# Attention and two gated layers on one core: casts and subtractions of converted weights put off behind the next step's split, and conversions moved between steps

## Chip, cores and metric

The kernel runs on one core of a Trainium2 chip. The metric is the device time of one execution in microseconds. The engines named below are PE (TensorE: matmuls), DVE (VectorE), ACT (ScalarE), POOL (GpSimd) and SP (SyncE, which issues DMAs).

## What is computed

Local attention feeds a gated layer, whose result feeds a second one with products in a row. All weights come as 64-bit floats; all arithmetic is float32.

```python
attn = softmax(masked(q @ k.T / sqrt(64))) @ v        # 4 x 8 heads x 576 x 64
x = attn.transpose(0, 2, 1, 3).reshape(2304, 512)
x = (silu(x @ w_gate) * (x @ w_val)) @ w_out          # d_ff = 1536
x = (((x @ w1) * (x @ w2)) @ w3) @ w_out2             # d_ff = 1024
```

## The kernel before

**Products.** A float32 value is held as two parts, `hi` (rounded, type fp32r) and `lo` (the rest). A product is the sum of three matmuls, hi x hi, hi x lo and lo x hi. `w3 @ w_out2` is multiplied out once (`fold_mm`) to a folded weight `fw`, so the second layer too is "up" products, an elementwise product and one "down" product.

**Slices and steps.** The features of both layers are cut into 20 slices of 128: slices 0 to 11 are the first layer's, 12 to 19 the second's. The 2304 tokens are cut into groups 0 to 3 of 512 and group 4 of 256. A step (c, g) is slice c with group g. On PE a step is the up product of (c, g), twice 12 matmuls into the banks `pa` and `pb`, and then the down product of the step before, 12 matmuls into the banks `po`. The down product of (c, g) so stands behind the up product of the step after. DVE multiplies `pr` = `pb` x `ga`, ACT having made `ga` from `pa` (silu, or a copy in the second layer); ACT casts `pr` to `sh`, POOL subtracts `sl` = `pr` - `sh` (`split_act`). The first matmul of the down product reads `sh`, the second `sl`. DVE adds the four `po` banks to `y` (`o` in the second layer). In slice 11 the sum is the next layer's input: DVE makes `total` or `y`, ACT casts it to `x_hi`, POOL subtracts `x_lo`. Slices 9, 10, 11 and 14 to 19 start with `pair`, which does groups 0 and 1 together with fewer matmuls, from sums of weights (`S`) and of inputs (`T`); its banks are `px`, `py`, `pz`, and `ca`, `cb`, `cc` are copies of them to which DVE adds.

**Conversions.** A weight block arrives as 64-bit words in `raw`; five DVE instructions make it a float32 block `val` (`to_f32`, lines 126, 128, 130, 133, 136: three TENSOR_SCALAR, two SCALAR_TENSOR_TENSOR). For a w3 block a transposition follows (L188). Then ACT casts the block to `whi` (L199) and POOL subtracts `wlo` (L200). `val` has two buffers, `raw` three, the slices' `whi` and `wlo` two each. For slice c there are three blocks, w0 and w1 for the two up products and w2 for the down product (from slice 12 on `fw`, which comes as float32 and needs no conversion); eight `wo` blocks and sixteen `w3` blocks serve the folds of slices 3 to 6.

**What sets the order.** The schedule is written by hand: each engine runs its instructions in the order in which they are recorded, and semaphores are set where one reads what another wrote. `plan(c)` says behind which step of slice c which block for the next slice is converted; `follow` records them after the step's up product, `pr`, split and the down product of the step before. So behind step (c, g) DVE has the adds of the down product, then the conversion; ACT has the cast; POOL the subtraction. Then comes step (c, g + 1) with `ga`, `pr`, `sh` and `sl`. The load of a block is issued by SP when the conversion two before it is recorded.

The main loop, and its core:

```python
            if n >= 2:
                if n >= GFILL:
                    up_mm(c, g)
                up_act(c, g)
            if behind:
                down(*behind.pop())
            behind = [(c, g)]
        if g != "pair":
            follow(c, g)
```

Of the kernel before, what the change touches and what calls it, by code (L numbers as in the profile page):

```python
# [9 lines left out]
F32 = mybir.dt.float32  # L10
# [4 lines left out]
ALU = mybir.AluOpType  # L15
# [20 lines left out]
def attention_ffn_kernel(  # L36
# [14 lines left out]
    nc = tc.nc  # L51
# [91 lines left out]
    def slice_tiles(c):  # L143
        if c not in whl:
            whl[c] = (wp.tile([P, WC], F32R, tag="whi", name=f"whi{c}", bufs=2),
                      wp.tile([P, WC], F32R, tag="wlo", name=f"wlo{c}", bufs=2))
        return whl[c]
# [29 lines left out]
    def job_run(job):  # L177
        kind, a, j = job
        if kind == "fw":
            val = raw_of.pop(job).bitcast(F32)[:, 0:PW]  # L180
        else:
            val = wp.tile([P, PW], F32, tag="wval", name=f"val_{kind}{a}_{j}", bufs=2)
            yield from to_f32(val, raw_of.pop(job))
        if kind == "w" and j < 2:
            val_of[a, j] = val
        if kind == "w3":
            turned = fold_pool[0].tile([P, PW], F32, tag="w3t", name=f"w3t{a}_{j}", bufs=1)
            nc.vector.transpose(out=turned, in_=val)  # L188
            hi = fold_pool[0].tile([P, PW], F32R, tag="w3h", name=f"w3h{a}_{j}", bufs=2)
            lo = fold_pool[0].tile([P, PW], F32R, tag="w3l", name=f"w3l{a}_{j}", bufs=2)  # L190
            nc.scalar.copy(out=hi, in_=turned)
            nc.gpsimd.tensor_tensor(out=lo, in0=turned, in1=hi.bitcast(F32), op=ALU.subtract)
            w3T[a, j] = hi, lo
            return
        if kind in ("w", "fw"):
            hi, lo = (t[:, j * PW:(j + 1) * PW] for t in slice_tiles(a))
        else:
            hi, lo = wo_hi[:, a, :], wo_lo[:, a, :]
        nc.scalar.copy(out=hi, in_=val)  # L199
        nc.gpsimd.tensor_tensor(out=lo, in0=val, in1=hi.bitcast(F32), op=ALU.subtract)  # L200

    val_of, fold_pool, folded = {}, [], []

# [6 lines left out]
    def plan(c):  # L210

        T = ("T", c)
        res = {g: [] for g in order_of(c)[:1] + ["after", "mid"] + order_of(c)[1:]}
        if c in PAIRS:

            res["pair"] = [("w" if c < NFT else "fw", c, 2)]
        if c + 1 == NCH:
            return res
        w0, w1, w2 = (("w", c + 1, j) for j in range(3))
        if c + 1 >= NFT:  # L220
            w2 = ("fw", c + 1, 2)
        if c == 0:

            res[4] = [w2]
        elif c < 3:

            res[0], res[3] = [w0, w1], [w2]
            wo = [("wo", j, 0) for j in range(NJ)]
            if c == 1:
                res[1], res[2], res[4] = wo[0:2], wo[2:3], wo[3:5]  # L230
            else:
                res[1], res[2], res[4] = wo[5:7], wo[7:8], [("w3", 0, 0)]
        elif c < 3 + NF2 // 2:
            f = 2 * (c - 3)
            res = {0: [("w3", f, 1), w0], 1: [("fold", f), ("w3", f + 1, 0), w1], 2: [("w3", f + 1, 1)],
                   3: [("fold", f + 1), w2], 4: [("w3", f + 2, 0) if f + 2 < NF2 else T]}
        elif c == PAIR0 - 2:
            res = {0: [w0, w1], 1: [T], 2: [], 3: [w2], 4: [T]}
        elif c == PAIR0 - 1:
            res = {0: [T], 1: [w0, T, T], 2: [w1, T], 3: [("S", c + 1)], 4: []}  # L240
        elif c == NFT - 1:
            res.update({"after": [w0], 3: [w1], 4: [w2]})
        elif c == PAIR1 - 2:
            res = {0: [T], 1: [w0, T], 2: [w1], 3: [w2], 4: [T]}
        elif c == PAIR1 - 1:
# [28 lines left out]
    def next_job():  # L274

        while not next(running):
            pass
# [310 lines left out]
    def up_act(c, g):  # L588
        pa, pb = upp.pop((c, g))
        up_val(c, g, up_gate(c, g, pa), pb)  # L590
# [192 lines left out]
    def down(c, g):  # L783
        (down1 if c < NFT else down2)(c, g)
# [22 lines left out]
    def half(g, k):  # L807
        return tuple(x[g][:, k * HK:(k + 1) * HK, :] for x in (x_hi, x_lo))
# [77 lines left out]
    def pair(c, between):  # L886
        whi, wlo = whl[c]
        shi, slo = ss.pop(c)

        def weights(j, k):  # L890
            return tuple(w[:, j * PW + k * HK * P:j * PW + (k + 1) * HK * P] for w in (whi, wlo))

        def sums(i):
            return shi[:, i - 1], slo[:, i - 1]

        def product(pt, a, b, first, last):
            terms = [(i, j, kk) for kk in range(HK) for i, j in ((0, 0), (1, 0), (0, 1))]
            for n, (i, j, kk) in enumerate(terms):
                nc.tensor.matmul(out=pt, lhsT=a[i][:, kk * P:(kk + 1) * P], rhs=b[j][:, kk, :],  # L899
                                 start=first and n == 0, stop=last and n == len(terms) - 1,  # L900
                                 skip_group_check=not (first and last))

        def snap(tag, src):
            t = pair_pool[0].tile([P, 512], F32, tag=tag, name=f"{tag}{c}", bufs=1)
            nc.scalar.copy(out=t, in_=src)
            return t

        def add(t, src):
            nc.vector.tensor_tensor(out=t, in0=src, in1=t, op=ALU.add)

        def silu(t):
            if c < NFT:
                nc.scalar.activation(out=t, in_=t, func=AF.Silu)

        def prod(g, gate, val):
            pr = sp.tile([P, 512], F32, tag="pr", name=f"pr{c}_{g}", bufs=2)
            nc.vector.tensor_tensor(out=pr, in0=val, in1=gate, op=ALU.mult)
            split_act(c, g, pr)

        x, y, z = bank("pa", f"px{c}", 2), bank("pb", f"py{c}", 2), bank("pa", f"pz{c}", 2)  # L920
        product(x, weights(0, 0), half(0, 0), True, False)
        product(y, weights(0, 1), half(0, 1), True, True)
        gate0 = snap("ca", x)
        add(gate0, y)
        if c < NFT:
            for _ in range(5):
                next(running)
        else:
            next_job()
        product(x, sums(2), xs[2], False, False)  # L930
        product(z, sums(1), half(1, 0), True, False)
        gate1 = snap("cb", x)
        silu(gate0)
        product(x, sums(3), xs[3], False, False)
        val1 = snap("cc", x)
        add(val1, z)
        if c < NFT:
            next_job()
        between()
        product(x, weights(1, 1), xs[4], False, True)  # L940
        prod(0, gate0, x)
        product(z, sums(4), half(1, 1), False, True)
        add(gate1, z)
        silu(gate1)
        prod(1, gate1, val1)
# [3 lines left out]
    def follow(c, g):  # L949
        for what, *args in plan(c)[g]:  # L950
            if what == "fold":
                fold_mm(*args)
            elif what == "S":
                s_sums(*args)
            elif what == "T":
                layer = args[0] >= NFT
                if layer not in sums_of_x:
                    sums_of_x[layer] = t_sums(int(layer))
                next(sums_of_x[layer])
            else:  # L960
                next_job()

    steps = [(c, g) for c in range(NCH) for g in order_of(c)]
    behind = []
    for n, (c, g) in enumerate(steps):
        if g == "pair":
            pair(c, lambda: down(*behind.pop()))
            follow(c, "after")
            behind = [(c, 0), (c, 1)]
        elif len(behind) == 2:  # L970
            gate, val = bank("pb", f"pb{c}_{g}", 2), bank("pa", f"pa{c}_{g}", 2)
            upp[c, g] = gate, val
            for j, pt in enumerate((gate, val)):
                for _ in up_product(c, g, j, pt):
                    pass
                if j == 0:
                    down(*behind.pop(0))
                    follow(c, "mid")
            up_act(c, g)
            down(*behind.pop())  # L980
            behind = [(c, g)]
        else:
            if n >= 2:
                if n >= GFILL:
                    up_mm(c, g)
                up_act(c, g)
            if behind:
                down(*behind.pop())
            behind = [(c, g)]
        if g != "pair":  # L990
            follow(c, g)
# [31 lines left out]
```

## Time and profile before

| | |
|---|---|
| median of 3 runs | 889.79 us (888.75 to 889.86) |
| profiled execution | 887.68 us, of which the span of instructions is 885.9 us |
| mean granted clock of PE | 0.994 |
| busy share: PE, DVE, POOL, ACT | 97%, 77%, 39%, 31% |
| chain that ended last | PE 73%, DVE 19% |

The span runs from the first to the last instruction; some 2 us of the execution lie around it. The profile's times are counted from the span's start. Attention takes the first 110 us; steps (0, 0) to (0, 3) have their up products inside it. Slice 1 starts on PE at 126.8 us, slice 3 at 211.7, slice 12 at 586. The granted clock is the share of TensorE's full 2.4 GHz; 0.50 is 1.2 GHz. Idle time of an engine stands in brackets with what ended it.

### The profile page before, as it was taken

The numbers are of one execution on the slowest core, as the hardware profiler recorded it, in microseconds if no ns is written. First come the engines' busy times: TensorE is split into PE (matmuls) and PEld (weight loads), VectorE is DVE, ScalarE is ACT, GpSimd is POOL, SyncE is SP. The second block draws the span as 40 slices with busy tenths as digits, with TensorE's granted clock in tenths as the row PEclk, the third lists the DMA queues.
The fourth block names the chain that finished last, engine by engine and source line by source line (L and its number), as shares of the span: only waits on it lengthen the run. The fifth ranks groups of instructions, "written<-read, shape, count | busy, mean of one in ns | idle before, by whom it ended". The sixth has DMA issues, their size and how long they took to land.

```text
span 885.9 us, 13578 instructions
## 1 busy us (share of the span) xinstructions
PE 861.3 (97%) x5138; PEld 714.1 (81%) x5138; DVE 679.4 (77%) x1151; ACT 272.5 (31%) x543; POOL 342.8 (39%) x323
## 2 busy tenths in 40 slices
PE   7899999999999999999999999999999999999998
PEld 5678778767888888888888888777788888888886
DVE  6998878888888787887887767779885675765745
ACT  6778422122222222122232222442232222222221
POOL 7676523333333323322223333585322423323331
PEclk9999999999999999999999999999999999999999
DMA  7988413233323333322101101101110110111014
GB/s 196 222 193 178 121 45 96 74 97 78 89 76 93 88 95 85 90 84 91 40 25 48 48 24 48 37 24 36 50 34 13 59 39 22 48 36 36 1 48 167
DMA packets 107857, 65.91 MB, mean 74 GB/s; under 512 B 71952, under 2 KB 100880, under 8 KB 107792
## 3 DMA queue, kind: packets, MB, share of 16 engines
q1 hardware_dynamic: 107248, 64.78, 27.0%
q8 instruction: 41, 0.67, 0.3%
q10 hardware_dynamic: 544, 0.26, 0.1%
q14 instruction: 24, 0.20, 0.1%
HBM read 58.20 MB, written 6.82 MB: 73 GB/s over the span
## 4 chain that ended last, share of the span: by engine, by line
PE 73%; DVE 19%; issue 3%; POOL 2%; ACT 2%; DMA 1%; SPq 0%; ACTq 0%; DVEq 0%; POOLq 0%
PE pa L567 17%; PE pb L567 17%; PE po L751 13%; PE po L778 10%; PE px L899 6%; PE fold L792 5%; PE pz L899 3%; DVE y L737 2%; PE py L899 1%; DVE val_w L130 1%; DVE y L758 1%; DVE val_w L133 1%; DVE mx L473 1%; DVE s L467 1%; DVE val_w L128 1%
## 5 line engine op out<-in xcount | busy, mean ns | idle before, releaser
L652 POOL TENSOR_TENSOR sl<-pr,sh 128x512 fp32r<-128x512 f32 (+1 forms) x98 | 115.6, 1180 | 175.1 <-ACT sh L651 175.1
L200 POOL TENSOR_TENSOR wlo<-val_w,whi 128x512 fp32r<-128x512 f32 x52 | 68.6, 1320 | 189.7 <-ACT whi L199 187.7
L737 DVE TENSOR_TENSOR y<-po,y 128x512 f32<-128x512 f32 (+1 forms) x200 | 114.9, 628 | 3.0 <-PE po L751 3.0
L567 PE MATMUL pb<-x_hi,wlo 128*128 128x512 f32 (+1 forms) x320 | 116.0, 365 | 0.9 <-POOL wlo L200 0.9
L567 PE MATMUL pb<-x_hi,whi 128*128 128x512 f32 (+1 forms) x320 | 116.0, 365 | 0.8 <-ACT whi L199 0.8
L644 DVE TENSOR_TENSOR pr<-pb,ga 128x512 f32<-128x512 f32 (+1 forms) x71 | 43.7, 616 | 94.9 <-ACT ga L583 40.3
L567 PE MATMUL pa<-x_hi,whi 128*128 128x512 f32 (+1 forms) x320 | 115.6, 364 | 0.0
L567 PE MATMUL pa<-x_hi,wlo 128*128 128x512 f32 (+1 forms) x320 | 115.4, 363 | 0.0
L567 PE MATMUL pb<-x_lo,whi 128*128 128x512 f32 (+1 forms) x320 | 103.8, 365 | 0.0
L567 PE MATMUL pa<-x_lo,whi 128*128 128x512 f32 (+1 forms) x320 | 103.0, 363 | 0.0
L651 ACT CAST sh<-pr 128x512 fp32r<-128x512 f32 (+1 forms) x98 | 56.6, 578 | 128.3 <-DVE pr L644 84.4
L751 PE MATMUL po<-sl,whi 128*128 128x512 f32 (+1 forms) x240 | 90.5, 377 | 4.1 <-POOL sl L652 4.1
L751 PE MATMUL po<-sh,whi 128*128 128x512 f32 (+1 forms) x240 | 90.1, 375 | 2.4 <-ACT sh L651 1.9
L751 PE MATMUL po<-sh,wlo 128*128 128x512 f32 (+1 forms) x240 | 89.8, 374 | 0.0
L199 ACT CAST whi<-val_w 128x512 fp32r<-128x512 f32 x52 | 32.3, 621 | 183.5 <-DVE val_w L136 183.5
L737 DVE TENSOR_TENSOR o<-po,o 128x512 f32<-128x512 f32 x126 | 80.8, 683 | 9.0 <-PE po L778 9.0
L567 PEld LDWEIGHTS pb<-x_hi,whi 128*128 128x128 f32 x320 | 60.8, 190 | 10.8 <-ACT whi L199 1.2
L567 PEld LDWEIGHTS pb<-x_hi,wlo 128*128 128x128 f32 x320 | 60.8, 190 | 10.7 <-POOL wlo L200 1.2
L567 PEld LDWEIGHTS pa<-x_hi,whi 128*128 128x128 f32 x320 | 60.5, 189 | 10.0
L567 PEld LDWEIGHTS pa<-x_hi,wlo 128*128 128x128 f32 x320 | 60.3, 189 | 9.9
L567 PEld LDWEIGHTS pb<-x_lo,whi 128*128 128x128 f32 x320 | 59.3, 190 | 9.4
L567 PEld LDWEIGHTS pa<-x_lo,whi 128*128 128x128 f32 x320 | 58.9, 188 | 9.5
(182 smaller groups left out, 1749.5 us busy)
## 6 DMA issues: line engine op xcount, KB each, us to landing
raw_w<-in_moe_w_dram SPq DMA_DIRECT2D x256, 32.0 KB, 1.9
raw_w<-in_moe_w_dram SPq DMA_DIRECT2D x16, 512.0 KB, 3.5
raw_w<-in_moe_w_gate_dram SPq DMA_DIRECT2D x12, 512.0 KB, 3.7
raw_w<-in_moe_w_val_dram SPq DMA_DIRECT2D x12, 512.0 KB, 3.7
raw_w<-in_moe_w_out_dram SPq DMA_DIRECT2D x12, 512.0 KB, 3.5
out_dram<-o SPq DMA_DIRECT2D x18, 256.0 KB, 2.1
raw_wo<-in_moe_w_out_dram SPq DMA_DIRECT2D x8, 512.0 KB, 3.5
vnear<-in_v_dram SPq DMA_DIRECT2D x32, 96.0 KB, 4.1
```

Of the source, the lines that this page charges most:

```text
L128: nc.vector.tensor_scalar(out=dst, in0=dst, scalar1=UP_LO, scalar2=UP_HI, op0=ALU.max, op1=ALU.min)
L199: nc.scalar.copy(out=hi, in_=val)
L200: nc.gpsimd.tensor_tensor(out=lo, in0=val, in1=hi.bitcast(F32), op=ALU.subtract)
L567: nc.tensor.matmul(out=pt[:, :n], lhsT=a[:, ws], rhs=tokens(x, kk, t0, n), start=i == 0, stop=i == len(terms) - 1)
L644: nc.vector.tensor_tensor(out=pr[:, :n], in0=pb[:, :n], in1=ga[:, :n], op=ALU.mult)
L651: nc.scalar.copy(out=sh[:, :n], in_=pr[:, :n])
L652: nc.gpsimd.tensor_tensor(out=sl[:, :n], in0=pr[:, :n], in1=sh[:, :n].bitcast(F32), op=ALU.subtract)
L737: nc.vector.tensor_tensor(out=dst, in0=src, in1=dst, op=ALU.add)
L751: nc.tensor.matmul(out=po[:, :n], lhsT=a[:, ws], rhs=x[:, :n], start=first, stop=last)
L778: nc.tensor.matmul(out=po, lhsT=x[:, ts], rhs=a[:, ws], start=first, stop=last)
L792: nc.tensor.matmul(out=pt, lhsT=a[:, j % HJ * P:(j % HJ + 1) * P], rhs=b[:, j, :], start=first and j == 0, stop=last and j == NJ - 1)
L899: nc.tensor.matmul(out=pt, lhsT=a[i][:, kk * P:(kk + 1) * P], rhs=b[j][:, kk, :], start=first and n == 0, stop=last and n == len(terms) - ...
```

## The change

Three things. In slices without `pair`, and for the conversion behind step (10, 4), the cast and the subtraction of a converted block are not recorded at once but put on a list (`pending`); `high_lows` records them after the next step's `up_act`, so behind its `ga`, `pr`, `sh` and `sl` (in `pair`, behind the first split). Blocks of w3 are cast at once as before. `plan` places conversions anew:

| step | before | now |
|---|---|---|
| (0, 4) | w2 | w2, wo 0 |
| (1, 0) to (1, 4) | w0 w1; wo 0, 1; wo 2; w2; wo 3, 4 | wo 1, w0; w1; wo 2; w2; wo 3, 4 |
| (2, 0) to (2, 4) | w0 w1; wo 5, 6; wo 7; w2; w3 | wo 5, w0; w1; wo 6; w2; wo 7, w3 |
| (10, 4) | none | w0 of slice 12 |
| slice 11: behind the pair; 3; 4 | w0; w1; fw | w1; none; fw |
| (13, 0) to (13, 2) | w0 T; w1 T T; T | T; w0 T T; w1 T |

```diff
--- before.py
+++ after.py
@@ -192,12 +192,26 @@
             nc.gpsimd.tensor_tensor(out=lo, in0=turned, in1=hi.bitcast(F32), op=ALU.subtract)
             w3T[a, j] = hi, lo
             return
-        if kind in ("w", "fw"):
-            hi, lo = (t[:, j * PW:(j + 1) * PW] for t in slice_tiles(a))
+
+        def high_low():
+            if kind in ("w", "fw"):
+                hi, lo = (t[:, j * PW:(j + 1) * PW] for t in slice_tiles(a))
+            else:
+                hi, lo = wo_hi[:, a, :], wo_lo[:, a, :]
+            nc.scalar.copy(out=hi, in_=val)
+            nc.gpsimd.tensor_tensor(out=lo, in0=val, in1=hi.bitcast(F32), op=ALU.subtract)
+
+        if put_off[0]:
+            pending.append(high_low)
         else:
-            hi, lo = wo_hi[:, a, :], wo_lo[:, a, :]
-        nc.scalar.copy(out=hi, in_=val)
-        nc.gpsimd.tensor_tensor(out=lo, in0=val, in1=hi.bitcast(F32), op=ALU.subtract)
+            high_low()
+
+
+    put_off, pending = [False], []
+
+    def high_lows():
+        while pending:
+            pending.pop(0)()
 
     val_of, fold_pool, folded = {}, [], []
 
@@ -221,15 +235,12 @@
             w2 = ("fw", c + 1, 2)
         if c == 0:
 
-            res[4] = [w2]
+            res[4] = [w2, ("wo", 0, 0)]
         elif c < 3:
 
-            res[0], res[3] = [w0, w1], [w2]
-            wo = [("wo", j, 0) for j in range(NJ)]
-            if c == 1:
-                res[1], res[2], res[4] = wo[0:2], wo[2:3], wo[3:5]
-            else:
-                res[1], res[2], res[4] = wo[5:7], wo[7:8], [("w3", 0, 0)]
+            rest = [("wo", j, 0) for j in range(1, NJ)] + [("w3", 0, 0)]
+            rest = rest[4 * (c - 1):4 * c]
+            res = {0: [rest[0], w0], 1: [w1], 2: [rest[1]], 3: [w2], 4: [rest[2], rest[3]]}
         elif c < 3 + NF2 // 2:
             f = 2 * (c - 3)
             res = {0: [("w3", f, 1), w0], 1: [("fold", f), ("w3", f + 1, 0), w1], 2: [("w3", f + 1, 1)],
@@ -239,13 +250,15 @@
         elif c == PAIR0 - 1:
             res = {0: [T], 1: [w0, T, T], 2: [w1, T], 3: [("S", c + 1)], 4: []}
         elif c == NFT - 1:
-            res.update({"after": [w0], 3: [w1], 4: [w2]})
+            res.update({"after": [w1], 4: [w2]})
         elif c == PAIR1 - 2:
             res = {0: [T], 1: [w0, T], 2: [w1], 3: [w2], 4: [T]}
         elif c == PAIR1 - 1:
-            res = {0: [w0, T], 1: [w1, T, T], 2: [T], 3: [("S", c + 1)], 4: []}
+            res = {0: [T], 1: [w0, T, T], 2: [w1, T], 3: [("S", c + 1)], 4: []}
         else:
             res.update({"mid": [w0], 2: [w1], 3: [("S", c + 1)]})
+            if c == NFT - 2:
+                res[4] = [("w", NFT, 0)]
         return res
 
     NOT_JOBS = ("fold", "S", "T")
@@ -939,6 +952,7 @@
         between()
         product(x, weights(1, 1), xs[4], False, True)
         prod(0, gate0, x)
+        high_lows()
         product(z, sums(4), half(1, 1), False, True)
         add(gate1, z)
         silu(gate1)
@@ -958,7 +972,9 @@
                     sums_of_x[layer] = t_sums(int(layer))
                 next(sums_of_x[layer])
             else:
+                put_off[0] = c not in PAIRS or (c, g) == (NFT - 2, 4)
                 next_job()
+                put_off[0] = False
 
     steps = [(c, g) for c in range(NCH) for g in order_of(c)]
     behind = []
@@ -977,6 +993,7 @@
                     down(*behind.pop(0))
                     follow(c, "mid")
             up_act(c, g)
+            high_lows()
             down(*behind.pop())
             behind = [(c, g)]
         else:
@@ -984,6 +1001,7 @@
                 if n >= GFILL:
                     up_mm(c, g)
                 up_act(c, g)
+            high_lows()
             if behind:
                 down(*behind.pop())
             behind = [(c, g)]
```

On ACT, in slice 1, before: `whi` and `wo_hi` are casts of converted blocks, `ga` and `sh` those of the steps, whose group is the number after the name.

```order
L199 CAST whi_2066<-val_w_2_2278 128x512
L583 ACTIVATE ga_0_2312<-pa_0_2286 128x512
L651 CAST sh_0_2316<-pr_0_2314 128x512
L199 CAST whi_2349<-val_w_0_2343 128x512
L199 CAST whi_2349<-val_w_1_2355 128x512
L583 ACTIVATE ga_1_2389<-pa_1_2363 128x512
L651 CAST sh_1_2393<-pr_1_2391 128x512
L199 CAST wo_hi<-val_wo_0_2419 128x512
L199 CAST wo_hi<-val_wo_0_2429 128x512
L583 ACTIVATE ga_2_2463<-pa_2_2437 128x512
```

And now:

```order
L596 ACTIVATE ga_0_2318<-pa_0_2292 128x512
L664 CAST sh_0_2322<-pr_0_2320 128x512
L201 CAST whi_2066<-val_w_2_2278 128x512
L201 CAST wo_hi<-val_wo_0_2286 128x512
L596 ACTIVATE ga_1_2393<-pa_1_2367 128x512
L664 CAST sh_1_2397<-pr_1_2395 128x512
L201 CAST wo_hi<-val_wo_0_2353 128x512
L201 CAST whi_2403<-val_w_0_2361 128x512
L596 ACTIVATE ga_2_2461<-pa_2_2435 128x512
L664 CAST sh_2_2465<-pr_2_2463 128x512
```

Each cast of a converted block has moved behind the next step's `ga` and `sh`; one `wo` cast stands in step (1, 0) that stood in (1, 1).

On POOL at the same place, before:

```order
L200 TENSOR_TENSOR wlo_2067<-val_w_2_2278,whi_2066 128x512
L652 TENSOR_TENSOR sl_0_2317<-pr_0_2314,sh_0_2316 128x512
L200 TENSOR_TENSOR wlo_2350<-val_w_0_2343,whi_2349 128x512
L200 TENSOR_TENSOR wlo_2350<-val_w_1_2355,whi_2349 128x512
L652 TENSOR_TENSOR sl_1_2394<-pr_1_2391,sh_1_2393 128x512
L200 TENSOR_TENSOR wo_lo<-val_wo_0_2419,wo_hi 128x512
L200 TENSOR_TENSOR wo_lo<-val_wo_0_2429,wo_hi 128x512
```

And now:

```order
L665 TENSOR_TENSOR sl_0_2323<-pr_0_2320,sh_0_2322 128x512
L202 TENSOR_TENSOR wlo_2067<-val_w_2_2278,whi_2066 128x512
L202 TENSOR_TENSOR wo_lo<-val_wo_0_2286,wo_hi 128x512
L665 TENSOR_TENSOR sl_1_2398<-pr_1_2395,sh_1_2397 128x512
L202 TENSOR_TENSOR wo_lo<-val_wo_0_2353,wo_hi 128x512
L202 TENSOR_TENSOR wlo_2404<-val_w_0_2361,whi_2403 128x512
L665 TENSOR_TENSOR sl_2_2466<-pr_2_2463,sh_2_2465 128x512
```

Two subtractions for weights, where a step had two conversions, now stand directly behind the next step's `sl`, where they stood ahead of it.

On DVE at the start of slice 11's pair, before (the last `y` is that of step (10, 4), `val_w_2` the conversion of the pair's own w2):

```order
L737 TENSOR_TENSOR y_2255<-po_3_2_6116,y_2255 128x512
L737 TENSOR_TENSOR y_2255<-po_3_3_6121,y_2255 128x512
L909 TENSOR_TENSOR ca_6141<-py_6127,ca_6141 128x512
L126 TENSOR_SCALAR val_w_2_6146<-raw_w_2_5947 128x512
L128 TENSOR_SCALAR val_w_2_6146<-val_w_2_6146 128x512
L130 TENSOR_SCALAR val_w_2_6146<-val_w_2_6146 128x512
L133 SCALAR_TENSOR_TENSOR val_w_2_6146<-raw_w_2_5947,val_w_2_6146 128x512
L136 SCALAR_TENSOR_TENSOR val_w_2_6146<-raw_w_2_5947,val_w_2_6146 128x512
L909 TENSOR_TENSOR cc_6173<-pz_6128,cc_6173 128x512
```

And now:

```order
L750 TENSOR_TENSOR y_2255<-po_3_2_6116,y_2255 128x512
L750 TENSOR_TENSOR y_2255<-po_3_3_6121,y_2255 128x512
L126 TENSOR_SCALAR val_w_0_6128<-raw_w_0_5947 128x512
L128 TENSOR_SCALAR val_w_0_6128<-val_w_0_6128 128x512
L130 TENSOR_SCALAR val_w_0_6128<-val_w_0_6128 128x512
L133 SCALAR_TENSOR_TENSOR val_w_0_6128<-raw_w_0_5947,val_w_0_6128 128x512
L136 SCALAR_TENSOR_TENSOR val_w_0_6128<-raw_w_0_5947,val_w_0_6128 128x512
L922 TENSOR_TENSOR ca_6149<-py_6135,ca_6149 128x512
L126 TENSOR_SCALAR val_w_2_6154<-raw_w_2_5999 128x512
L128 TENSOR_SCALAR val_w_2_6154<-val_w_2_6154 128x512
L130 TENSOR_SCALAR val_w_2_6154<-val_w_2_6154 128x512
L133 SCALAR_TENSOR_TENSOR val_w_2_6154<-raw_w_2_5999,val_w_2_6154 128x512
```

Five instructions for `val_w_0`, w0 of slice 12, stand ahead of `ca` and of the conversion of w2.

## Rows read from the trace of the kernel before

**Rows 1.** Page, part 1: busy time of each engine, share of span.
```profile
PE 861.3 (97%) x5138; PEld 714.1 (81%) x5138; DVE 679.4 (77%) x1151; ACT 272.5 (31%) x543; POOL 342.8 (39%) x323
```

**Rows 2.** Busy time by stretch: slices 1-2, half clock, slice 7, slice 12.
```profile
core 0: us, PE busy (x) PEld busy (x) DVE busy (x) ACT busy (x) POOL busy (x), PEclk, DMA share, GB/s
126.79:211.68 84.89, 79.41 (x361) 64.74 (x360) 71.38 (x122) 18.32 (x32) 29.07 (x23) 0.96 0.28 85
181.50:184.91 3.41, 3.41 (x9) 2.67 (x8) 3.27 (x6) 0.62 (x1) 0.81 (x1) 0.50 0.15 30
418.97:455.97 37.00, 37.00 (x182) 31.35 (x181) 29.37 (x42) 10.66 (x17) 8.49 (x8) 1.00 0.10 29
585.95:628.83 42.88, 39.98 (x182) 32.30 (x180) 36.33 (x49) 13.75 (x26) 25.14 (x20) 0.96 0.14 44
```

**Rows 3.** Waits of PE in slices 1 and 2: total us, times, longest us.
```profile
PE po L751 <- POOL sl L652: 3.6, 5, 0.9
PE po L751 <- ACT sh L651: 1.9, 2, 1.1
```

**Rows 4.** DVE timeline, slice 1: start, us, instruction, [idle before <- its end].
```profile
127.60 0.42 DVE L126 TENSOR_SCALAR val_w<-raw_w 128x512 int32<-128x512 int32 x1
...
132.53 0.69 DVE L644 TENSOR_TENSOR pr<-pb,ga 128x512 f32<-128x512 f32 x1 [2.14 <-POOL wlo L200]
...
142.91 0.69 DVE L644 TENSOR_TENSOR pr<-pb,ga 128x512 f32<-128x512 f32 x1 [1.18 <-ACT ga L583]
...
149.53 1.48 DVE L130 TENSOR_SCALAR val_wo<-val_wo 128x512 int32<-128x512 int32 x1
...
153.65 0.69 DVE L644 TENSOR_TENSOR pr<-pb,ga 128x512 f32<-128x512 f32 x1 [1.18 <-ACT ga L583]
154.26 2.47 DVE L737 TENSOR_TENSOR y<-po,y 128x512 f32<-128x512 f32 x4
156.65 0.42 DVE L126 TENSOR_SCALAR val_wo<-raw_wo 128x512 int32<-128x512 int32 x1
...
160.62 0.69 DVE L644 TENSOR_TENSOR pr<-pb,ga 128x512 f32<-128x512 f32 x1 [1.18 <-ACT ga L583]
```

**Rows 5.** Timeline of ACT, slice 1, end of step 2.
```profile
159.47 0.62 ACT L199 CAST wo_hi<-val_wo 128x512 fp32r<-128x512 f32 x1 [4.42 <-DVE val_wo L136]
160.00 0.59 ACT L583 ACTIVATE ga<-pa 128x512 f32<-128x512 f32 x1
```

**Rows 6.** Timeline of POOL, slice 1.
```profile
149.43 1.29 POOL L200 TENSOR_TENSOR wo_lo<-val_wo,wo_hi 128x512 fp32r<-128x512 f32 x1 [3.75 <-ACT wo_hi L199]
...
162.10 1.27 POOL L652 TENSOR_TENSOR sl<-pr,sh 128x512 fp32r<-128x512 f32 x1 [0.63 <-ACT sh L651]
```

**Rows 7.** Timeline of DVE, where slice 3 begins.
```profile
218.40 0.71 DVE L188 STREAM_TRANSPOSE w3t<-val_w 128x512 f32<-128x512 f32 x1
220.35 0.69 DVE L644 TENSOR_TENSOR pr<-pb,ga 128x512 f32<-128x512 f32 x1 [1.24 <-ACT ga L583]
```

**Rows 8.** Timeline of PE: second matmul of down(3,0).
```profile
224.25 0.39 PE L751 MATMUL po<-sl,whi 128*128 128x512 f32 x1
```

**Rows 9.** Timeline of PE, step (12,0).
```profile
589.62 0.50 PE L567 MATMUL pb<-x_hi,whi 128*128 128x512 f32 x1 [0.79 <-ACT whi L199]
590.97 0.70 PE L567 MATMUL pb<-x_hi,wlo 128*128 128x512 f32 x1 [0.85 <-POOL wlo L200]
```

**Rows 10.** Timeline of DVE, slice 11.
```profile
552.45 0.69 DVE L909 TENSOR_TENSOR ca<-py,ca 128x512 f32<-128x512 f32 x1 [1.18 <-PE py L899]
...
557.17 0.69 DVE L909 TENSOR_TENSOR cc<-pz,cc 128x512 f32<-128x512 f32 x1 [1.32 <-ACT cc L905]
...
562.84 0.42 DVE L126 TENSOR_SCALAR val_w<-raw_w 128x512 int32<-128x512 int32 x1
...
584.63 1.40 DVE L128 TENSOR_SCALAR val_w<-val_w 128x512 f32<-128x512 f32 x1
586.06 1.40 DVE L130 TENSOR_SCALAR val_w<-val_w 128x512 int32<-128x512 int32 x1
```

## The prediction

> **What bounds the kernel now.** I read the page's busy times first, then the idle gaps of PE, then the engine that ends each gap. PE is busy 97% of the span [rows 1], so only PE's gaps can be won. I looked for them by comparing slices. Slice 7 has no gap at full clock: 37.00 us for its five steps [rows 2]. Slices 1 and 2 hold the same matmuls twice and take 84.89 us instead of 74.00: 10.9 us lost. Slice 12 takes 42.88: 5.9 us lost [rows 2]. In slices 1 and 2 PE waits for `sl` and `sh`, the split of the activations, 3.6 and 1.9 us [rows 3]; the rest is matmuls at half clock (two stretches like the one of 3.41 us at 0.50 [rows 2], some 1.7 us each; PE had stood still twice just before) and matmuls' refill after a gap. In slice 12 PE waits for `whi` and `wlo` of the weights (0.79 and 0.85 us [rows 9]); the rest of its 5.9 is half clock again, and two waits for `sl` in steps 2 and 3.
>
> Why is `sl` late? DVE is the slower engine there. A step with one conversion takes DVE 6.97 us from one `pr` to the next (153.65 to 160.62), a step with two 10.74 (142.91 to 153.65) [rows 4]. A PE step is 37.00 / 4.5 = 8.2 us, so the steps with two conversions put DVE behind. The last 1.18 us before each `pr` are idle, ended by `ga` [rows 4]: ACT stood at the cast of the converted weight, which waits for the conversion's last instruction, and only then did `ga` (cast at 159.47, `ga` at 160.00, `pr` at 160.62 [rows 4, 5]). And in a step with two conversions, L130 of the second takes 1.48 us (L126, as wide, takes 0.42 alone) while POOL subtracts the first: it ends at 151.01, 0.29 after POOL's 150.72 [rows 4, 6].
>
> **The change, part by part.** *Deferred casts.* From the rows: `pr` to the adds 0.61, four adds 2.39 (154.26 to 156.65), one conversion 10.74 - 6.97 - 1.05 = 2.72. `sl` is ready 2.75 after `pr` (162.10 + 1.27 - 160.62 [rows 4, 6]). Now ACT does `ga` early, so the 1.18 go. What comes instead: the subtractions of the step before stand behind `sl` on POOL, the first until 4.05 after `pr`, a second until 5.3 (1.29 each [rows 6]), and the next conversion starts at 3.0, in the middle of them. I price this by L130's row: the held instruction ends 0.29 after POOL's. Also a conversion's buffer is the one of two conversions ago, so after a step with two it must wait until the first subtraction is through. Time of a DVE step then:
> - one put off, one conversion: 4.05 + 0.29 + 2.27 = 6.6 (before 6.97);
> - two put off, one conversion: 5.3 + 0.29 + 2.27 = 7.85;
> - two put off, two conversions, as in step 0: 7.85 + 2.72 = 10.55 (before 10.38, from 132.53 to 142.91 [rows 4]);
> - the half-wide step 4 with one put off and two conversions: `sl` is about half as long, so 8.2 (before about 10.5, the 10.74 less half a `pr`).
>
> So the wait that goes is mostly given back to POOL; the gain is 0.4 in a plain step, 2.3 in step 4, and what follows from the new places.
>
> *New places in slices 0 to 2.* One conversion moves from slice 1 into step (0,4), where DVE waited 2.14 us before `pr` [rows 4]: `pr` of (1,0) comes at 127.60 + 2 x 2.72 = 133.05 instead of 132.53, and its down product is 6 us away, so this costs nothing. Slice 1 is then 10.55 + 7.85 + 6.6 + 6.6 + 8.2 = 39.8. Slice 2 is 10.55 + 7.85 + 6.6 + 6.6, and its step 4, with the first w3 block behind a wo block, 8.2 + 0.8 for the transposition [rows 7] + 1.3 (the cast of w3 is not put off, so `ga` still waits for it, 218.40 + 0.64 to 220.35 [rows 7]) = 10.3; together 41.9. `pr` of (3,0) comes at 133.05 + 81.7 = 214.8; before it came at 220.35 [rows 7], 5.6 later. There `sl` was ready at 223.10 and PE used it at 224.25 [rows 8], 1.15 of slack; now PE waits for it, at 217.55. PE is thus 6.7 us earlier at this point. The fold behind it needs the second w3 block from 223.3 on (twelve matmuls of the down product, twelve of the fold, two more, 0.23 each). That block's conversion starts at 216.7, is held by `sl` and by a put-off subtraction until 219.3, and with its last three instructions, transposition, cast and subtraction, 4.6 in all, is ready at 223.9: 0.6 late. Gain 6.1; 4.8 of the 10.9 stay, as waits for `sl` at about (2,1), (2,3) and (3,0). A stretch at half clock at (2,1) would hide in the later waits; one at (3,0) would cost up to 1.7 (half of 3.41 [rows 2]).
>
> *Slices 3 to 8.* Casts of w0, w1, w2 move behind the next split. PE has no gap there now, DVE loses one `ga` wait of 1.18 and gets one hold of 0.9 per conversion, about even, and the slack of `sl` holds: nothing.
>
> *Slices 10 to 13.* w0 of slice 12 is converted in (10,4), ahead of `ca` in the pair. Its 2.72 fill the 1.18 that DVE idles before `ca` and the 1.32 before `cc` [rows 10], so `cc` comes 0.2 late and `pr` behind it, which waits for PE, on time. If it were not so, 2.72 would be the bound. w1 takes w0's old place behind the pair. There L126 (562.84 [rows 10]) now meets w0's subtraction and waits for its end, one instruction's 0.46, so `total` starts 0.5 us late, which PE sees once: -0.5 (between 0 and a full hold of 1.05). The five instructions around 585 leave DVE, where two of them took 1.40 each behind POOL's run of `x_lo` [rows 10]: 2.72 + 2 x 0.97 = 4.7 us. The weights that PE waited for at 589.62 and 590.97 [rows 9] are there some 20 us earlier, and slice 12's two waits for `sl` go, since DVE wins 4.7 and PE comes only 3.3 earlier. All 5.9 go; less 0.5, that is 5.4. In slice 13 two conversions stand a step later each, as they do in slice 8, where PE has no gap: nothing. The loads on SP's queue follow the order of the conversions, two conversions ahead as before; no count of instructions or DMAs changes.
>
> *Sum.* 6.1 + 5.4 = 11.5 off the profiled execution's 887.68 gives 876.2. The median of the timed runs, 889.79, stands 2.1 above it, so I forecast **878.3**. With 1.7 for a half clock, and 1 us either way on ten steps of DVE, 876 to 881.
>
> The hold of DVE by POOL is where a rule bears on this change. The row: 1.48 instead of 0.43, for a TENSOR_SCALAR [rows 4]. The Trainium skill ("SBUF — State Buffer", Who interferes with whom) calls the port pair that the two engines share an exclusive lock, kept for a whole instruction by whoever issued first, and counts DVE instructions with two SBUF inputs in, so L133 and L136 too. The trace agrees for TENSOR_SCALAR; no row that I read shows L133 or L136 held. By it all five instructions of a conversion are exposed to a subtraction that moves among them, not three, which is rival D's way; the sum above, which counts one hold each, stays as it is.
>
> **The rivals.** *B, the wait only changes its name.* If holds and buffers cost 0.4 us more per put-off subtraction (14 of them up to (3,0)), they eat the 5.6, and only slices 10 to 13 gain: 889.8 - 5.4 = 884.4. For it: my own steps with two put off are no shorter than before. Against: a conversion moved off slice 1, and step 4 gains by itself.
>
> *C, the holds do not bite.* If the conversions run beside the subtractions, DVE needs 5.7 per plain step and all 10.9 go too: 889.8 - 10.9 - 5.4 = 873.5. Against: every overlap in the rows is held.
>
> *D, slower.* Subtractions standing back to back hold one DVE instruction each: at 584.63 and 586.06 two in a row took 1.40 [rows 10]. If each of the 14 holds a second one (0.97), DVE's path grows by 13.6, `pr` of (3,0) comes at 228.4, and PE is 6.9 late there instead of 6.7 early; less 5.4, and with one more stretch of half clock, 889.8 + 6.9 - 5.4 + 1.7 = 893.0. It turns slower from 11.5 / 14 = 0.8 us per subtraction. Against: in a plain step `sl` is done before the conversion starts, and one subtraction is all that is left.
>
> *E, no difference:* B holds, and the pair pays the full 2.72 for w0 and as much again at (11,2) for w1, which gives slice 12's 5.4 back: 889.8. Against: the idle time beside `ca` and `cc` [rows 10].
>
> **How the numbers follow.** Forecast 0.60, B 0.16, C 0.12, D 0.06, E 0.06. About 0.2% (1.8 us) is what a measurement of this kernel can tell from no change. Forecast, B and C are faster by more: 0.88. E is the same: 0.06. D is slower: 0.06. The range from 873.0 to 884.5 holds the forecast, C and the better half of B, and leaves out D, E and the rest of B, 0.2.
>
> **What would show it.** In the changed profile `pr` in slices 1 and 2 should wait no more for `ga`; the first instruction of a conversion should take about 1.3 us or wait for POOL; the stretch from slice 1's first matmul to slice 3's should be some 77 us instead of 84.89, with 2.4 of new waits at the start of slice 3; slice 12 should take 37, with no wait for `whi` or `wlo`. I am wrong if DVE's steps with one conversion are not about 6.6 long, if waits of PE turn up in slices 3 to 6, or if slice 11 gets longer by more than 1 us.

## The result and the profile after

The changed kernel takes 878.25 us (median of 4 runs, 877.95 to 879.09) against 889.27 (888.22 to 889.86) for the kernel before on the same chip: ratio 0.9879, 95% interval 0.9862 to 0.9896. A second submission of the same code gave 878.97 (878.47 to 879.24), ratio 0.9889 [0.9874, 0.9903]. The forecast was 878.3, faster.

The profiled execution of the first submission took 879.09 us, the slowest of its four, and its span is 877.2. The page's busy times, beside [rows 1]:

```profile
PE 856.6 (98%) x5138; PEld 711.4 (81%) x5138; DVE 688.5 (78%) x1151; ACT 270.2 (31%) x543; POOL 338.2 (39%) x323
```

Busy time by stretch in this trace: slices 1 and 2, slice 3, then slices 11 and 12 (beside [rows 2]; the first two numbers are the stretch and its length, PEclk is the granted clock):

```profile
core 0: us, PE busy (x) PEld busy (x) DVE busy (x) ACT busy (x) POOL busy (x), PEclk, DMA share, GB/s
127.46:203.98 76.52, 74.92 (x361) 62.62 (x360) 68.65 (x116) 17.04 (x32) 27.34 (x22) 1.00 0.28 87
203.98:254.99 51.01, 49.19 (x230) 40.12 (x228) 46.32 (x75) 11.83 (x22) 17.71 (x15) 1.00 0.36 91
...
544.65:582.19 37.54, 36.93 (x176) 29.93 (x175) 30.90 (x43) 16.00 (x28) 24.67 (x21) 1.00 0.11 36
582.19:620.08 37.89, 37.31 (x182) 31.24 (x180) 33.63 (x44) 12.57 (x24) 19.45 (x19) 1.00 0.11 35
```

The same cuts in the trace of before, and in two other traces that the text comes back to, give this table (each length is one stretch from a slice's first matmul on PE to the next one's):

| stretch, us | before | change | change, second trace | e8 |
|---|---|---|---|---|
| slice 1 starts at | 126.79 | 127.46 | 127.76 | 128.33 |
| slices 1 to 3 | 133.00 | 127.53 | 127.57 | 123.07 |
| slices 4 to 10 | 289.66 | 289.66 | 289.66 | 289.66 |
| slice 11 | 36.50 | 37.54 | 37.51 | 36.94 |
| slice 12 | 42.88 | 37.89 | 37.00 | 37.00 |
| from slice 13 on | 257.07 | 257.12 | 257.10 | 257.00 |
| span | 885.9 | 877.2 | 876.6 | 872.0 |

So the gain is where it was looked for: 5.4 to 5.5 us in slices 1 to 3 and, net, 3.9 to 4.9 in slices 11 and 12, while slices 4 to 10 keep their length to the hundredth. Slice 1 starts 0.7 to 1 us later in the traces of the change; the spans contain that, the stretches don't. It starts at 127.39 in the trace of e4 too, whose order up to slice 9 is that of before, so 0.6 us of this come and go without the change.

What is left of PE's waits in slices 1 to 3, from its timeline:

```profile
185.53 0.50 PE L764 MATMUL po<-sh,whi 128*128 128x512 f32 x1 [0.41 <-ACT sh L664]
186.89 0.50 PE L764 MATMUL po<-sl,whi 128*128 128x512 f32 x1 [0.85 <-POOL sl L665]
201.31 0.50 PE L764 MATMUL po<-sl,whi 128*128 128x512 f32 x1 [0.34 <-POOL sl L665]
216.82 0.50 PE L764 MATMUL po<-sh,whi 128*128 128x512 f32 x1 [0.34 <-ACT sh L664]
218.17 0.50 PE L764 MATMUL po<-sl,whi 128*128 128x512 f32 x1 [0.85 <-POOL sl L665]
224.63 0.50 PE L805 MATMUL fold<-wo_hi,w3l 128*128 128x512 f32 x1 [0.46 <-POOL w3l L192]
246.96 0.50 PE L805 MATMUL fold<-wo_hi,w3l 128*128 128x512 f32 x1 [0.18 <-POOL w3l L192]
```

Waits stay at (2,1), (2,3), (3,0) and the fold, the four places that the prediction names, and one at a later fold. No stretch at half clock is left in them: PEclk is 1.00 in all four windows.

### The profile page after: what moved, and what is told of

It is laid out like the page before. It is cut to its first block, busy times and chain, and to the rows that moved or that the text cites. A ratio compares the mean times of both kernels' runs of the same rounds, so it can differ in the third digit from the quotient of the medians.

```text
span 877.2 us, 13579 instructions
## 1 busy us (share of the span) xinstructions
PE 856.6 (98%) x5138; PEld 711.4 (81%) x5138; DVE 688.5 (78%) x1151; ACT 270.2 (31%) x543; POOL 338.2 (39%) x323
## 4 chain that ended last, share of the span: by engine, by line
PE 71%; DVE 19%; issue 3%; SPq 2%; POOL 2%; ACT 1%; DMA 1%; DVEq 0%; POOLq 0%; ACTq 0%
PE pa L580 16%; PE pb L580 16%; PE po L764 12%; PE po L791 10%; PE px L912 6%; PE fold L805 4%; PE pz L912 3%; DVE y L750 2%; SPq L172 2%; DVE val_w L133 2%; DVE val_w L126 1%; PE py L912 1%; DVE val_w L130 1%; DVE mx L486 1%; DVE val_w L128 1%
```

## The experiments

Each is told against the kernel before in its own submission (888.56 us for e1 to e4, 888.82 for e0 and e6 to e8, 888.93 for e5, e9 and e10). The diffs are against the changed kernel.

**e0, the change again**, unedited, so that later runs have it on their chip.

> The change itself once more, on the same chip and with the same runs of the kernel before as e6, e7 and e8, so that these can be compared with it: 878, 1.2% faster than before.

Measured: 878.97, ratio 0.9889 [0.9874, 0.9903]; its trace is the third column of the table.

**e1, the casts and subtractions put off, the plan of before.**

```diff
-            res[4] = [w2, ("wo", 0, 0)]
+            res[4] = [w2]
...
-            res.update({"after": [w1], 4: [w2]})
+            res.update({"after": [w0], 3: [w1], 4: [w2]})
...
-                put_off[0] = c not in PAIRS or (c, g) == (NFT - 2, 4)
+                put_off[0] = c not in PAIRS
```

(and slices 1, 2, 10 and 13 of the plan as before.)

> Casts and subtractions put off, all conversions in their old places. My theory (DVE's path from pr of (1,0) to pr of (3,0) sets the end of slices 1 and 2, each step's length being what pr, adds, conversions and the holds by POOL add up to): steps with two put off and two conversions 10.55, with two and one 7.85, plain 6.6, step 4 8.2; pr of (3,0) comes 85 us after pr of (1,0), where it was 87.8 before and is 81.7 with the change. PE gains some 3.5 us in slices 1 to 3 and 1 to 2 in slice 12, the wait for whi and wlo in (12,0) stays: 884 to 885. Rival, the new places do it all: 889, no change. Rival, putting off does it all: 878.

**e2, the new plan, casts and subtractions at once** (but for (10, 4), whose conversion needs it).

```diff
-                put_off[0] = c not in PAIRS or (c, g) == (NFT - 2, 4)
+                put_off[0] = (c, g) == (NFT - 2, 4)
```

> Conversions in their new places, casts and subtractions recorded at once as before (but for the one behind (10,4), whose buffer needs it). My theory: DVE idles 1.2 us before each pr for ga again, steps 6.97 with one conversion and 10.4 to 10.7 with two, pr of (3,0) 84.5 us after pr of (1,0) which itself is 2 us later; PE gains 2 us in slices 1 to 3, and 3 to 4 in slices 11 and 12 since w0 and w1 of slice 12 are early: 883 to 885. Rival, the new places do it all: 878. Rival, putting off does it all: 889.

Measured: e1 885.2, ratio 0.9962 [0.9948, 0.9976]; e2 884.84, ratio 0.9954 [0.9939, 0.9969]. On DVE the two parts add up: from `pr` of (1,0) to `pr` of (3,0) it takes 87.8 us before, 85.3 in e1 (132.66 to 217.97), 84.1 in e2 (137.09 to 221.23) and 81.7 with both. On PE they don't: slices 1 to 3 take 131.97 us in e1 (126.92 to 258.89) and 132.22 in e2 (128.48 to 260.70), 1.0 and 0.8 less than before (3.5 and 2 were expected), and 5.5 less with both. The reason in e2 stands in DVE's timeline of step (0,4) and the start of slice 1:

```profile
132.91 1.48 DVE L130 TENSOR_SCALAR val_wo<-val_wo 128x512 int32<-128x512 int32 x1
...
137.09 0.69 DVE L657 TENSOR_TENSOR pr<-pb,ga 128x512 f32<-128x512 f32 x1 [1.24 <-ACT ga L596]
```

With the casts at once, the conversion added to (0,4) is held by the subtraction of the first (1.48 instead of 0.43), and `ga` waits behind its cast. So `pr` of (1,0) comes 8.6 us after slice 1's first matmul (before 5.7, with both parts 6.2), and most of what the places win is spent there. In e1 it is the step with two conversions behind two put-off subtractions that keeps coming back (10.56, 10.57 and 10.53 us). And behind the last two of its waits, for `sh` and `sl` of (2,3), PE runs at half clock (granted clock 0.63 from 206 to 210): from the second wait's end at 206.62 it needs 4.21 us to slice 3, where the same matmuls take 2.67 in the change (201.31 to 203.98). So 1.5 of the 2.5 that DVE wins go there. In slice 12 the places do most: it takes 38.28 us in e2 and 41.27 in e1, against 42.88 before. e1 also leaves the wait for `whi` in slice 12, as its PE timeline shows, beside [rows 9]:

```profile
588.69 0.50 PE L581 MATMUL pb<-x_hi,whi 128*128 128x512 f32 x1 [0.76 <-ACT whi L201]
```

**e3, the change in slices 0 to 8 alone; e4, in slices 10 to 13 alone.** e3 has the plan of before from slice 10 on and `put_off[0] = c < PAIR0`. e4 has the plan of before in slices 0 to 2 and

```diff
-                put_off[0] = c not in PAIRS or (c, g) == (NFT - 2, 4)
+                put_off[0] = NFT <= c < PAIR1 or (c, g) == (NFT - 2, 4)
```

> The change in slices 0 to 8 alone; slices 9 to 13 as before. My theory: the part of slices 1 to 3 is worth 5.5 to 6 us, the two parts add up: 883.5. If the two parts are not independent (a half clock or a wait that one leaves and the other takes), the gains of this run and of the next do not add up to the change's 11.

> The change in slices 10 to 13 alone; slices 0 to 9 as before. My theory: the loss of slice 12 goes (5.9 us), less 1.0 that slice 11 loses and 0.9 that stays as a wait for sl in (12,3): 4 us, 885. Slices 1 and 2 take 84.9 us on PE as before.

Measured: e3 883.5, ratio 0.9938 [0.9924, 0.9953], so 5.1 us; e4 883.81, ratio 0.9944 [0.993, 0.9959], so 4.8 us. In e4's trace slices 1 to 3 take 133.03 us, slice 11 37.51 and slice 12 37.00; the wait for `sl` in (12,3) that was expected to stay isn't there. The two halves add up to 9.8 of the 9.9 (e0) to 11.0 (first submission) that the whole wins: they are independent, unlike e1 and e2.

**e5, each put-off subtraction of slices 0 to 2 done twice on POOL.** It doubles the one cost that rivals B, C and D differ about, and leaves everything else. `where[0]` is the slice behind whose step the conversion is recorded.

```diff
+        twice = put_off[0] and where[0] < 3
...
             nc.gpsimd.tensor_tensor(out=lo, in0=val, in1=hi.bitcast(F32), op=ALU.subtract)
+            if twice:
+                nc.gpsimd.tensor_tensor(out=lo, in0=val, in1=hi.bitcast(F32), op=ALU.subtract)
```

> The change, with each put-off subtraction of slices 0 to 2 done twice on POOL (the second writes the same again). If DVE is held by POOL, the dose must show: a plain step (one put off, one conversion) becomes longer than 6.6 by what a second subtraction holds, 0.5 if DVE gets in between the two (then a second instruction is held, 0.97, or half of it) up to 1.27 if it does not; the steps with two put off by 1.3 to 2.5. On ten steps 10 to 16 us more on DVE's path, of which PE sees nearly all: 888 to 895, and about 3 us of half clock may join. Rival, the conversions run beside the subtractions and the gain comes from ga alone: 878, no change.

Measured: 894.38 (893.62 to 895.28), ratio 1.0061 [1.0046, 1.0076], slower than before. DVE's timeline of step (1,0), then POOL's:

```profile
134.55 0.68 DVE L661 TENSOR_TENSOR pr<-pb,ga 128x512 f32<-128x512 f32 x1
...
139.92 1.50 DVE L126 TENSOR_SCALAR val_wo<-raw_wo 128x512 int32<-128x512 int32 x1 [3.35 <-POOL wlo L206]
141.45 1.40 DVE L128 TENSOR_SCALAR val_wo<-val_wo 128x512 f32<-128x512 f32 x1
...
147.40 0.68 DVE L661 TENSOR_TENSOR pr<-pb,ga 128x512 f32<-128x512 f32 x1
```

```profile
135.97 1.30 POOL L669 TENSOR_TENSOR sl<-pr,sh 128x512 fp32r<-128x512 f32 x1 [8.41 <-ACT sh L668]
137.22 1.30 POOL L204 TENSOR_TENSOR wlo<-val_w,whi 128x512 fp32r<-128x512 f32 x1
138.59 1.29 POOL L206 TENSOR_TENSOR wlo<-val_w,whi 128x512 fp32r<-128x512 f32 x1
139.84 1.30 POOL L204 TENSOR_TENSOR wo_lo<-val_wo,wo_hi 128x512 fp32r<-128x512 f32 x1
141.22 1.36 POOL L206 TENSOR_TENSOR wo_lo<-val_wo,wo_hi 128x512 fp32r<-128x512 f32 x1
```

The step takes 12.85 us instead of the change's 10.49. Both ways of losing show: DVE's L126 waits 3.35 us until both subtractions of the buffer's old block are through, then L126 and L128 are held one after the other, each ending 0.27 to 0.28 us after a subtraction of POOL. Over both slices, `pr` of (1,0) to `pr` of (3,0), 134.55 to 231.30, it takes 96.75 us against 81.67: 15.1 for 14 more subtractions, 1.08 each, and the time is 15.4 above e0's. POOL is only 39% busy, yet here each of its subtractions is on DVE's path, and through it on PE's.

**e6, the put-off subtractions of slices 0 to 2 on DVE,** behind the step's adds; **e7, that of (10, 4) alone; e8, both.**

```diff
+        on_dve = put_off[0] and where[0] < 3
...
+            if on_dve:
+                lows.append((lo, val, hi))
+                return
             nc.gpsimd.tensor_tensor(out=lo, in0=val, in1=hi.bitcast(F32), op=ALU.subtract)
...
+    def low_parts():
+        while lows:
+            lo, val, hi = lows.pop(0)
+            nc.vector.tensor_tensor(out=lo, in0=val, in1=hi.bitcast(F32), op=ALU.subtract)
...
     def follow(c, g):
+        low_parts()
```

In e7 the condition is `where[0] == NFT - 2`, in e8 either.

> The change, but the put-off subtractions of slices 0 to 2 are made by DVE, behind the adds of the next step, instead of POOL. My theory: the hold and the wait for the buffer go, 0.62 per subtraction comes: plain steps 6.3, steps with two put off and one conversion 6.95, with two and two 9.1, step 4 8.8; pr of (3,0) comes 77 us after pr of (1,0) instead of 81.7, earlier than PE needs it. The waits for sl at (2,1), (2,3) and (3,0) go, 4.3 us: 874. Rival, DVE has no room for 15 more instructions (9.4 us): no change, or slower, 878 to 883.

> The change, but the put-off subtraction of w0 of slice 12 is made by DVE behind the pair's second pr instead of by POOL ahead of it. In the changed profile that pr took 1.72 instead of 0.69, both its inputs being in SBUF while POOL subtracts w0. My theory: that hold goes (-1.03), 0.62 comes, the conversion behind it is held once as before; total of (11,0) starts 0.4 to 1.0 earlier and PE's waits in down(11,1) shrink from 1.6 us to about 1: 877.5, at the edge of what can be measured, so the profile decides. Rival, the hold of pr is chance and not POOL's: pr still takes 1.72.

> e6 and e7 together: the put-off subtractions of slices 0 to 2 and that of w0 of slice 12 are DVE's. 873.5 if the two add up; if DVE has no room for them, no faster than the change's 878.

Measured: e6 874.9 (873.71 to 875.01), ratio 0.984 [0.9826, 0.9855]; e7 877.92 (877.36 to 878.72), 0.9878 [0.9861, 0.9894]; e8 873.92 (872.83 to 874.03), 0.983 [0.9815, 0.9844]. e8 beats both kernels. DVE's timeline of a step with two put-off subtractions and one conversion in e6:

```profile
144.32 0.68 DVE L667 TENSOR_TENSOR pr<-pb,ga 128x512 f32<-128x512 f32 x1
...
147.31 0.68 DVE L220 TENSOR_TENSOR wo_lo<-val_wo,wo_hi 128x512 fp32r<-128x512 f32 x1
147.91 0.68 DVE L220 TENSOR_TENSOR wlo<-val_w,whi 128x512 fp32r<-128x512 f32 x1
148.51 0.42 DVE L126 TENSOR_SCALAR val_w<-raw_w 128x512 int32<-128x512 int32 x1
...
151.22 0.68 DVE L667 TENSOR_TENSOR pr<-pb,ga 128x512 f32<-128x512 f32 x1
```

A subtraction costs DVE 0.60 us when DVE does it itself, from start to start, and the conversion behind it runs unheld: the step takes 6.90 instead of 7.87. The busy times by stretch of e8 show no loss left in slices 1 and 2 (74.00 is twice slice 7's 37.00 in [rows 2]); slices 3 and 11 are in the table above:

```profile
128.33:202.33 74.00, 74.00 (x361) 62.68 (x360) 71.86 (x133) 18.19 (x34) 11.23 (x10) 1.00 0.28 91
```

Against e0's trace that is 4.50 in slices 1 to 3 and 0.57 in slice 11, together 5.07, and the medians differ by 5.05 (the two profiled executions by 4.65, since slice 1 starts 0.57 later in e8's). e7's 1.05 against e0 can't be told from nothing by the intervals; its trace has slice 11 at 36.96 us (545.36 to 582.32), 0.55 shorter.

**e9, `T` of slice 12 one step later; e10, e8 and e9 together.** My theory was that DVE's sum for `T`, held by POOL in step (12,0) of the change's first trace, makes the last wait of slice 12 there.

```diff
-            res = {0: [T], 1: [w0, T], 2: [w1], 3: [w2], 4: [T]}
+            res = {0: [], 1: [w0, T], 2: [w1, T], 3: [w2], 4: [T]}
```

> The change, with the first sums of inputs of slice 12 (three DVE instructions, T) moved from step (12,0) to (12,1), the second ones from (12,1) to (12,2). In the changed profile the first of them took 3.71 instead of 1.2, standing beside POOL's four x_lo of group 4, and PE waits 0.86 for sl in (12,3). Theory, that hold is the cause: the three take 3.6 together, pr of (12,1) comes 2.5 earlier, no wait is left: 877.7, and the profile's rows decide. Rival, DVE is simply full there: the second sums now stand behind a held conversion in (12,2), and the wait moves to the next step and stays, 878.5 to 880.

> e8 and e9 together, as a candidate for the fastest version: 873 if e9 wins its 0.9 us, 874 to 875 if it does not.

Measured: e9 880.29 (879.92 to 881.97), ratio 0.9909 [0.9892, 0.9925]; e10 876.16 (874.97 to 876.51), 0.9853 [0.9839, 0.9868], 2.2 more than e8. Moving `T` wins nothing. In e9 slice 12 takes 39.07 us (582.02 to 621.09), because step (12,2) now has w1 and three sums of 1.22, as DVE's timeline shows:

```profile
604.14 0.68 DVE L657 TENSOR_TENSOR pr<-pb,ga 128x512 f32<-128x512 f32 x1
...
615.94 0.69 DVE L657 TENSOR_TENSOR pr<-pb,ga 128x512 f32<-128x512 f32 x1 [1.66 <-ACT ga L598]
```

11.8 us for one step where PE takes 8.2: PE waits 0.94 for `sh` and 0.61 for `sl` at 617 and 618. That is the way of the rival on record: the second sums stand behind a held conversion (L126 at 607.13 takes 1.25), and the wait moves. Since e9 puts longer waits in the place of the first trace's, it doesn't decide what made that one.

## Why the prediction was right, and where its sizes were off

**What bounds the kernel: right.** Only PE's gaps gave time. The slices without a gap kept their length, the stretches at half clock went with the waits before them, and e5 shows the chain from POOL through DVE to PE from the other side.

**The length of DVE's steps: right to 0.1 us.** Predicted 10.55, 7.85, 6.6, 6.6 and 8.2 in slice 1, and in slice 2 the same with 10.3 at the end. `pr` in the change's timeline:

```profile
133.70 0.68 DVE L657 TENSOR_TENSOR pr<-pb,ga 128x512 f32<-128x512 f32 x1
...
137.69 1.49 DVE L126 TENSOR_SCALAR val_wo<-raw_wo 128x512 int32<-128x512 int32 x1 [1.99 <-POOL wlo L202]
...
144.19 0.69 DVE L657 TENSOR_TENSOR pr<-pb,ga 128x512 f32<-128x512 f32 x1
...
152.06 0.68 DVE L657 TENSOR_TENSOR pr<-pb,ga 128x512 f32<-128x512 f32 x1
155.05 1.31 DVE L126 TENSOR_SCALAR val_wo<-raw_wo 128x512 int32<-128x512 int32 x1
158.66 0.68 DVE L657 TENSOR_TENSOR pr<-pb,ga 128x512 f32<-128x512 f32 x1
...
165.25 0.42 DVE L657 TENSOR_TENSOR pr<-pb,ga 128x256 f32<-128x256 f32 x1
173.52 0.68 DVE L657 TENSOR_TENSOR pr<-pb,ga 128x512 f32<-128x512 f32 x1
...
215.37 0.69 DVE L657 TENSOR_TENSOR pr<-pb,ga 128x512 f32<-128x512 f32 x1 [1.18 <-ACT ga L596]
```

Measured 10.49, 7.87, 6.60, 6.59, 8.27, then 10.57, 7.81, 6.60, 6.58, 10.29; in sum 81.67 where 81.7 was forecast. `pr` no longer waits for `ga` as in [rows 4]; instead L126 waits for the buffer and is held (1.99 and 1.49 in step (1,0)), or only held (1.31). `pr` of (3,0) still waits, as forecast, because the cast of w3 isn't put off. The hold in step (1,0) ends at 139.18, 0.28 after the end of POOL's second put-off subtraction (the prediction took 0.29):

```profile
137.62 1.28 POOL L202 TENSOR_TENSOR wo_lo<-val_wo,wo_hi 128x512 fp32r<-128x512 f32 x1
```

That is the trade which the prediction priced: the wait is mostly given back to POOL.

**Slices 1 to 3: 6.1 forecast, 5.4 to 5.5 measured.** PE uses `sl` of (3,0) 90.7 us after slice 1's first matmul; before it was 97.5 ([rows 8] less 126.79), and 6.7 was the forecast of the difference. So up to there the forecast is met. Behind it 1.3 us go instead of the 0.6 forecast for the fold. PE's timeline shows where, beside the rows at 218.17, 224.63 and 246.96 above; matmuls otherwise start 0.23 apart:

```profile
218.50 0.40 PE L764 MATMUL po<-sh,wlo 128*128 128x512 f32 x1
...
223.79 0.39 PE L805 MATMUL fold<-wo_lo,w3h 128*128 128x512 f32 x1
...
246.40 0.39 PE L805 MATMUL fold<-wo_lo,w3h 128*128 128x512 f32 x1
```

The fold loses 0.61 (223.79 to 224.63, less 0.23), as foreseen. Not foreseen were the second fold's wait, 0.33 (246.40 to 246.96, less 0.23), and some 0.1 behind each of the three waits, where the next matmul starts 0.33 or 0.34 later (at 218.50, 224.97 and 247.30).

**Slice 12: 5.9 forecast, 5.88 in the second trace, 4.99 in the first.** It takes 37.00 in e0's, e4's and e8's traces. The first trace has one wait more (0.58 for `sl` at 617.67), and its slice 12 is 0.89 longer; the e9 section above shows that moving `T` doesn't win it back. What differs is who got through first. DVE's first sum for `T` and POOL's `x_lo` beside it, first trace:

```profile
591.43 3.71 DVE L836 TENSOR_TENSOR t<-x_hi,x_hi 128x1024 f32<-128x1024 f32 x1
```

```profile
591.17 0.79 POOL L776 TENSOR_TENSOR x_lo<-total,x_hi 128x256 fp32r<-128x256 f32 x1
591.87 2.19 POOL L776 TENSOR_TENSOR x_lo<-y,x_hi 128x256 fp32r<-128x256 f32 x3
```

And in e0's, the same code:

```profile
591.79 1.58 DVE L836 TENSOR_TENSOR t<-x_hi,x_hi 128x1024 f32<-128x1024 f32 x1
```

```profile
591.54 0.75 POOL L776 TENSOR_TENSOR x_lo<-total,x_hi 128x256 fp32r<-128x256 f32 x1
592.24 5.09 POOL L776 TENSOR_TENSOR x_lo<-y,x_hi 128x256 fp32r<-128x256 f32 x3
```

Once DVE stands through four subtractions, once POOL's next ones stand through DVE's sums. The kernel before and e1 to e8 show the second way (1.42 to 1.62 for that sum). That the first way makes the wait at 617.67 is likely, since the wait is in neither e0's, e4's nor e8's trace, but no run shows it by itself.

**Slice 11: 0.5 forecast, 1.0 measured. This term came out at twice its size.** The prediction let w0's subtraction hold the first instruction of the next conversion, L126 at 562.84 in [rows 10], for 0.46, and said that `pr` behind `cc` comes on time. It does, but it is what is held; L126 behind it (559.07) takes 0.41, as if alone. DVE's timeline before, in the change and in e7, then POOL's in the change:

```profile
562.23 0.69 DVE L917 TENSOR_TENSOR pr<-cc,cb 128x512 f32<-128x512 f32 x1 [0.77 <-POOL sl L652]
```

```profile
557.42 1.72 DVE L930 TENSOR_TENSOR pr<-cc,cb 128x512 f32<-128x512 f32 x1 [0.77 <-POOL sl L665]
```

```profile
558.13 0.69 DVE L940 TENSOR_TENSOR pr<-cc,cb 128x512 f32<-128x512 f32 x1 [0.77 <-POOL sl L675]
```

```profile
557.30 1.29 POOL L202 TENSOR_TENSOR wlo<-val_w,whi 128x512 fp32r<-128x512 f32 x1
```

This `pr` of the pair reads `cc` and `cb`, both in SBUF, where the other `pr` shown read one bank of PSUM. It takes 1.72 instead of 0.69, everything behind it, `total` too, comes 1.0 later, and slice 11 grows by as much, the upper end of the 0 to 1.05 that the prediction allowed. In e7, with that subtraction on DVE, `pr` takes 0.69 and slice 11 is 0.55 shorter, although DVE now spends 0.60 on the subtraction. So this hold is the whole of the 1.0, and the hold of L126 that was forecast didn't come. The Trainium skill ("SBUF — State Buffer", Who interferes with whom) says that a DVE instruction with two SBUF inputs contends with a GpSimd one that reads SBUF, and that whoever issued first keeps the shared ports; these rows agree (POOL began at 557.30, DVE at 557.42). The prediction cited the rule for L133 and L136 and didn't ask which other instructions it covers. It also said that no row it read showed those two held. The trace of before has such a row, in the attention, beside a POOL instruction that began at 35.27 and took 0.94:

```profile
35.55 1.20 DVE L133 SCALAR_TENSOR_TENSOR val_w<-raw_w,val_w 128x512 int32<-128x512 int32 x1
```

**The sum.** 11.5 was forecast; the stretches give 5.4 + 5.9 - 1.0 = 10.3 in the second trace and 5.5 + 5.0 - 1.0 = 9.5 in the first. The medians differ by 11.0 in one submission and 9.9 in the other. So the sum was some 1.2 too large, 0.7 of it in slices 1 to 3 and 0.5 in slice 11. That 878.3 fell on the first median is luck. The prediction expected 876.2 for the profiled execution and added the 2.1 by which the median of the kernel before stood above its profiled one. The change's two profiled executions took 879.09 and 878.47, 2.9 and 2.3 more than expected. In the first, the median stood 0.8 below the profiled execution instead of 2.1 above, and these 2.9 cancelled the miss. What makes executions of the same code differ so is not shown.

**The signs of being wrong.** Of the three that the prediction named, one held off: DVE's steps with one conversion are 6.6 long. The other two came, each by little. Slice 11 got longer by 1.04 and 1.01 us, where more than 1 was the sign, and in slice 3 a wait turned up that wasn't forecast, 0.18 at the second fold. They mark the two terms that were mis-sized, and leave the mechanism of the gain as it was told.

**The rivals.** B is out: the steps came as priced. C's time, 873.5, is about what e8 reaches (873.92), but by taking the subtractions off POOL, not because they don't hold. D's price is real: e5's 1.08 us per additional subtraction is above D's threshold of 0.8, and made the kernel slower than before. D didn't come about because a single subtraction per block leaves one hold per step. E is out by e4.

## What to carry to other kernels

When a GpSimd instruction is moved away from one VectorE instruction, look at what it will stand beside next, and price every VectorE instruction there that reads two SBUF operands or is a TENSOR_SCALAR like those of the conversions: here each such meeting cost about 1 us (1.08 in e5, 1.03 for `pr` in slice 11), more than the 0.60 that VectorE needs to do the subtraction itself, so a mostly idle GpSimd was the wrong place for it. Two parts of a change whose gains add up on the late engine need not add up on the one that sets the end: alone, they won 1.0 and 0.8 us in slices 1 to 3, together 5.5. And take the slack from the traces stretch by stretch, with a slice that has no gap as the measure, since that told before any run how much there was to win.

## What the runs showed of the hardware beyond what was expected

- A subtraction on POOL beside DVE's conversions costs DVE 1.08 us (15.1 us for 14 in e5), by a hold or by the buffer that it keeps; the same subtraction on DVE costs 0.60 (e6).
- A DVE instruction held by POOL isn't always let in at the end of POOL's instruction: at 591.43 one was held 3.71 us through four subtractions in a row, while in e0's trace of the same code it got in after the first (1.58), and POOL stood instead (5.09 for three that take 2.19).
- A wait costs PE some 0.26 us more than the profile lists as idle, at full granted clock: at 224.63 it lists 0.46, and the starts at 223.79, 224.63 and 224.97, instead of 0.23 apart, lose 0.72; at 246.96 it lists 0.18, and 0.44 are lost.
